# Where an extra weight row's transfers stand in the DMA queue: between the last two pieces of w2 instead of ahead of all of w2

## The chip, the cores and the metric

The kernel runs on one core of one Trainium2 chip. The metric is the device time of one execution in microseconds (us). A profile records one further execution: when each instruction ran on each engine (PE is TensorE, DVE VectorE, ACT ScalarE, POOL GpSimd, SP SyncE), when each DMA packet ran, and when each transfer's semaphore was incremented.

## The reference

One decoding step for two sequences (B = 2, one token each, model width D = 576), an attention branch and a squared-ReLU branch that read the same normalised input:

```python
x = A_x
xn = _layernorm(x, axis=-1)
return x + _A_ref(xn, k_cache, v_cache, wq, wo) + _B_ref(xn, w1, b1, w2, b2)

# _A_ref: 32 query heads on 16 key/value heads of width 128, the last W = 2048 of 8192 cached positions
p = softmax((x @ wq) k^T * Dh ** -0.5);  o = p v;  return o @ wo
# _B_ref: F = 4608
h = relu(x @ w1 + b1) ** 2;  return h @ w2 + b2
```

Everything is bfloat16. The inputs are about 54 MB, and each byte is read once: 8 tiles of k and 8 of v of 2 MB each, wq, wo and w1 of about 5 MB each, and w2 of 5 MB.

## The kernel before

**Tiles.** Loads go to tiles of 128 partitions, each partition getting one contiguous run of memory. The k and v caches come in 8 units each (`load_k(u)`, `load_v(u)`, lines 106 and 107). w2 has 4608 rows of 576. It is taken as two halves (`x=2`) of 128 partitions with 18 rows each (`FR` = 18), so that w2's row r of half x on partition p meets the transposed hidden vector `hT_sb[:, x, r, :]`:

- `w2a` is the first half, all 18 rows (line 441).
- `w2b` holds rows 0 to 8 of the second half (line 442).
- `w2c` holds rows 9 to 16 of the second half. It comes in three transfers that `W2P` lists: rows 9 to 13 (720 KB), 14 and 15 (288 KB), and 16 (144 KB) (line 444).
- `w2x_sb` holds row 17 of the second half: 128 partitions of 1152 B. This is "the extra row". It has a tile of its own that is free from the start, and it is loaded in four transfers by partitions, listed in `XS`: 85, 13, 21 and 9 of them (line 440).

**The output.** All products add up in one PSUM tile, `out_ps`, by `out_acc` (four matmuls of 144 columns each on four row groups of TensorE, line 217). The order at the end of the program on PE is fixed by program order: the last attention units, the 32 products with `wo`, the product with the extra row (line 450), the 18 products with `w2a`, then those with `w2b` and `w2c` in the order of rows. The last has `stop=True`. ACT then copies `out_ps` out (line 458) and issues the output transfer (line 459).

**The DMA queues.** Nearly all loads are issued by SP, in program order, on one queue. Each transfer is split over DMA engines, of which there are 16, and each engine works through its share of the queue in order. x, b1, b2 and the output go through ACT's queue. b1 (8 rows of 1152 B) is one transfer: `for i in range(0, 2 * NG4, 8)` runs once (line 416).

**The waits.** The tile framework hands out eight DMA semaphores in turn, over the transfers of SP and ACT together, in program order: x, k_0, b1, b2, wq, k_1, v_0, k_2, v_1, k_3 and so on. A transfer is not issued before the transfer that had its semaphore eight places earlier has landed. It also waits until the tile that it overwrites is no longer read. While SP waits for one transfer, the transfers behind it wait too. At the end of the program this gives:

- the first three pieces of the extra row wait for v_4, k_6 and v_5, the fourth for nothing new (w1)
- w2a waits for k_7, w2b for v_6, and w2c's three pieces for v_7, wo and the first piece of the extra row
- the output transfer waits for the second piece of the extra row

Of the kernel before, what the change touches and what calls it, by code (L numbers as in the profile page):

```python
# [16 lines left out]
def kernel(  # L17
# [14 lines left out]
    nc = tc.nc  # L32
    P = 128
    B, Sq, D = A_x.shape
# [26 lines left out]
    NG4 = 4  # L61
# [12 lines left out]
    FR = L1 // P  # L74
    assert HW == 32 * FR and QH * 2 == NC and NC * WC == 32
    W2P = [(0, 9), (9, 14), (14, 16), (16, 17)]
    XS = [(0, 85), (85, 98), (98, 119), (119, 128)]
    BS = 16
    MB = BS * (B - 1) + 1
    RM = 32 * (NG4 - 1) + MB  # L80
# [12 lines left out]
    def matmul(*a, **k):  # L93
        tc.keep_in_program_order(nc.tensor.matmul(*a, **k))  # L94
# [28 lines left out]
    w2x_sb = const.tile([P, D], BF16, name="w2x_sb")  # L123
# [57 lines left out]
    for t0, half, k0, n, pc in ((0, 0, 0, NK, 0), (0, 1, 0, NK, 1), (1, 0, 1, NK - 1, 1), (1, 1, 0, NK - 1, 0)):  # L181
# [11 lines left out]
                          in_=own[:].unsqueeze(2).to_broadcast([P, NC, WC]))  # L193
# [11 lines left out]
                          in_=ident[0:2 * NG4, 0:2 * NG4].rearrange("p (x g) -> p x g", g=NG4).unsqueeze(3)  # L205
                          .to_broadcast([2 * NG4, 2, NG4, B]))

    b1_sb = const.tile([2 * NG4, HW], BF16, name="b1_sb")
    w2_rows = B_w2.rearrange("(x p r) n -> x p (r n)", x=2, r=FR)
# [5 lines left out]
    def out_acc(lhsT, rhs, o, start=False, stop=False):  # L215
        for i in range(4):
            matmul(out_ps[32 * i:32 * i + MB, :], lhsT=lhsT, rhs=rhs[:, o * D + i * OQ:o * D + (i + 1) * OQ],
                   start=start, stop=stop, skip_group_check=True, tile_position=(0, 32 * i))
# [91 lines left out]
    hT_sb = const.tile([P, 2, FR, MB], BF16, name="hT_sb")  # L310
# [75 lines left out]
    def step(u):  # L386
        fin = None
        w = u - 2
        with_pv = w >= 0
        for g in range(NG):  # L390
            transposes(u, g)
            if with_pv and g == 1:
                pv(w, 0, 2)
            if with_pv and g == 2:
                pv(w, 1, 2)
                fin = pv_end(w)
            if g == TG + 1:
                scores(u, 0)
            if g == TG + 2 and fin:
                fin()  # L400
        scores(u, 1)
        softmax(u)
# [10 lines left out]
    softmax(0)  # L413
    load_v(2)
    b1_rows = B_b1.rearrange("(x n) -> x n", n=HW)
    for i in range(0, 2 * NG4, 8):
        nc.scalar.dma_start(out=b1_sb[i:i + 8, :], in_=b1_rows[i:i + 8, :])
    nc.scalar.dma_start(out=xb_sb[B:B + 1, :], in_=B_b2.rearrange("(o n) -> o n", o=1))
    step(1)
    load_k(4)  # L420
# [15 lines left out]
    r9 = W2P[0][1]  # L436
    w2b_sb = kvpool.tile([P, r9 * D], BF16, tag="kv", name="w2b")
    w2c_sb = w2pool.tile([P, (FR - 1 - r9) * D], BF16, name="w2c")
    for p0, p1 in XS:
        nc.sync.dma_start(out=w2x_sb[p0:p1, :], in_=w2_rows[1, p0:p1, (FR - 1) * D:FR * D])  # L440
    nc.sync.dma_start(out=w2a_sb[:], in_=w2_rows[0])
    nc.sync.dma_start(out=w2b_sb[:], in_=w2_rows[1, :, 0:r9 * D])
    for r0, r1 in W2P[1:]:
        nc.sync.dma_start(out=w2c_sb[:, (r0 - r9) * D:(r1 - r9) * D], in_=w2_rows[1, :, r0 * D:r1 * D])
    step(NU - 1)
    pv_all(NU - 2)
    pv_all(NU - 1)
    for r in range(WR):
        out_acc(ws[:, r, :], wo_sb, r)
    out_acc(hT_sb[:, 1, FR - 1, :], w2x_sb, 0)  # L450
    for r in range(FR):
        out_acc(hT_sb[:, 0, r, :], w2a_sb, r)
    for r in range(FR - 1):
        w, o = (w2b_sb, r) if r < r9 else (w2c_sb, r - r9)
        out_acc(hT_sb[:, 1, r, :], w, o, stop=(r == FR - 2))

# [33 lines left out]
```

## Time and profile before

| | |
|---|---|
| median of 4 runs | 134.81 us (134.71 to 135.36) |
| the profiled execution | 135.36 us |
| its span, first to last instruction | 132.9 us |
| PE busy | 86.2 us, 65% |
| DVE busy | 63.2 us, 48% |
| ACT busy | 46.8 us, 35% |
| queue q1 (SP's loads), share of 16 engines | 3618 packets, 53.61 MB, 95.1% |
| queue q8 (instructions) | 7 packets, 0.11 MB, 0.3% |
| queue q10 (ACT's transfers) | 34 packets, 0.02 MB |
| HBM read over the span | 403 GB/s |
| SP issues the extra row | 96.0 to 97.4 us |
| SP issues w2a, w2b | 97.44, 100.80 us |
| SP issues w2c's three pieces | 105.6 to 117.8 us |
| ACT starts the copy-out | 130.09 us |

The profiled execution's own time is 2.5 us longer than its span: that lies around the first and last instruction. Queue q1's share of 95.1% says that the 16 DMA engines were reading for nearly the whole span. Among the waits of SP's queue toward the end, 11.4 us are for the landing of wo and 3.0 and 4.5 us for v tiles. PE's busy time spreads over the span, and in its last part PE mostly waits for one tile of weights after another.

### The profile page before, as it was taken

Reading aid. Unit: us, or ns where it says so; the run is one execution under the profiler, and the core shown is the slowest. Engines: PE = TensorE matmul, PEld = TensorE weight load, DVE = VectorE, ACT = ScalarE, POOL = GpSimd, SP = SyncE. Lnnn points to the kernel's source line nnn. Section 1 sums busy time; section 2 is a strip of 40 time slices with the busy share of each in tenths; the row PEclk is TensorE's granted clock in tenths of the full one; section 3 lists DMA queues with packets and bytes.
Section 4 is the critical chain, followed back from the end, with each engine's and each line's share of the span. In section 5 each row is a group of like instructions: output and inputs, shape, how many; then the busy total and the mean of one; then the engine's idle time right before and its main releaser. Section 6 shows DMA issues by size and latency. Waiting matters only on the chain.

```text
span 132.9 us, 2286 instructions
## 1 busy us (share of the span) xinstructions
PE 86.2 (65%) x949; PEld 53.1 (40%) x949; DVE 63.2 (48%) x176; ACT 46.8 (35%) x67; POOL 4.9 (4%) x15
## 2 busy tenths in 40 slices
PE   0079329599688697598887697205739971659461
PEld 0069302296344353454443363003337530138350
DVE  7754400355567496547596557410165766530000
ACT  5715400339376193436174445200206632000000
POOL 5000000010000100100100100100000001000000
PEclk9999955959999999689999779855686999555955
DMA  4999899999999999999999999989999998999960
GB/s 158 394 437 522 366 404 409 459 404 439 422 439 429 439 424 419 444 414 444 414 434 431 434 431 524 442 349 414 429 434 429 435 493 377 365 406 406 414 250 1
DMA packets 3661, 53.76 MB, mean 404 GB/s; under 512 B 441, under 2 KB 708, under 8 KB 964
## 3 DMA queue, kind: packets, MB, share of 16 engines
q1 hardware_dynamic: 3618, 53.61, 95.1%
q8 instruction: 7, 0.11, 0.3%
q10 hardware_dynamic: 34, 0.02, 0.0%
q14 instruction: 2, 0.02, 0.0%
HBM read 53.62 MB, written 0.00 MB: 403 GB/s over the span
## 4 chain that ended last, share of the span: by engine, by line
DMA 72%; PE 19%; DVE 2%; ACT 2%; issue 1%; SPq 0%; POOL 0%; ACTq 0%; DVEq 0%; POOLq 0%
DMA v<-in_A_v_cache_dram 26%; DMA w2c<-in_B_w_dram 17%; DMA k<-in_A_k_cache_dram 16%; DMA wq<-in_A_wq_dram 13%; PE kT_ps L97 10%; PE sc_ps L94 3%; PE q_ps L94 3%; PE o_ps L94 1%; PE out_ps L94 1%; ACT kT L269 1%; DVE m L290 1%; DVE qrow L237 1%; DVE kT L271 1%; PE op_ps L94 1%; SPq L106 0%
## 5 line engine op out<-in xcount | busy, mean ns | idle before, releaser
L97 PE MATMUL kT_ps<-ident_f,k 128*128 128x128 f32 x256 | 42.0, 316 | 5.7 <-DMA k<-in_A_k_cache_dram 4.4
L97 PEld LDWEIGHTS kT_ps<-ident_f,k 128*128 128x128 f32 x256 | 33.4, 162 | 19.2 <-issue 10.4
L269 ACT COPY kT<-kT_ps 128x1024 bf16<-128x1024 bf16 x32 | 31.9, 1012 | 19.1 <-PE kT_ps L97 19.0
L271 DVE COPY kT<-kT_ps 128x1024 bf16<-128x1024 bf16 x32 | 21.8, 681 | 6.4 <-PE kT_ps L97 6.1
L94 PE MATMUL sc_ps<-kT,qz 128*32 128x512 bf16 x128 | 9.7, 383 | 6.6 <-DVE kT L271 4.7
L301 ACT ACTIVATE p<-sc_ps,bias 128x512 bf16<-128x512 f32 x8 | 5.5, 687 | 21.4 <-DVE gown L297 18.2
L94 PE MATMUL o_ps<-v,pT 128*32 128x512 bf16 x128 | 12.1, 462 | 0.0
L94 PEld LDWEIGHTS <-xnT 128*4 128x4 bf16 x108 | 3.5, 121 | 15.8 <-issue 14.1
L94 PE MATMUL h_ps<-w,xnT 128*4 128x288 bf16 x72 | 4.4, 438 | 7.1 <-DMA w<-in_B_w_dram 7.1
L304 DVE STREAM_TRANSPOSE pT<-p 128x512 bf16<-128x512 bf16 x8 | 5.7, 710 | 6.1 <-ACT p L301 6.1
L334 DVE SCALAR_TENSOR_TENSOR o<-o_ps,in_s,o 128x128 f32<-128x128 f32 x24 | 8.3, 344 | 0.4
L290 DVE TENSOR_REDUCE m<-sc_ps 128x1 f32<-128x512 f32 x8 | 5.5, 691 | 4.6 <-PE sc_ps L94 4.6
L94 PE MATMUL q_ps<-wq,xnT 128*4 128x512 bf16 x36 | 4.0, 627 | 4.6 <-DMA wq<-in_A_wq_dram 4.6
L374 DVE TENSOR_TENSOR hrow<-t 100x1152 bf16<-100x1152 f32 x2 | 2.6, 1356 | 8.8 <-ACT t L372 8.8
L294 POOL PARTITION_ALL_REDUCE gmax<-m x8 | 2.9, 366 | 105.1 <-DVE m L292 105.1
L458 ACT CAST fin_sb<-out_ps 113x144 bf16<-113x144 f32 x1 | 0.3, 279 | 18.4 <-PE out_ps L94 18.4
L94 PE MATMUL op_ps<-o,of_h 128*32 128x129 f32 x16 | 3.7, 316 | 4.6 <-DVE o L334 4.6
L94 PEld LDWEIGHTS <-qz 128*32 128x32 bf16 x128 | 2.1, 94 | 10.3 <-DVE kT L271 7.2
L97 PE MATMUL pro_ps<-ident,xn_sb 2*128 2x2 bf16 x5 | 0.9, 181 | 6.8 <-DVE xn_sb L172 6.5
L332 DVE TENSOR_SCALAR o<-o_ps,in_s 128x128 f32<-128x128 f32 x8 | 2.7, 343 | 5.0 <-PE o_ps L94 5.0
L94 PEld LDWEIGHTS <-hT_sb 128*17 128x17 bf16 x144 | 3.3, 106 | 4.2 <-issue 4.2
L94 PE MATMUL out_ps<-wo,ws 128*17 128x144 bf16 x128 | 4.0, 324 | 1.2 <-DVE ws L350 1.2
(72 smaller groups left out, 55.7 us busy)
## 6 DMA issues: line engine op xcount, KB each, us to landing
k<-in_A_k_cache_dram SPq DMA_DIRECT2D x8, 2048.0 KB, 21.7
v<-in_A_v_cache_dram SPq DMA_DIRECT2D x8, 2048.0 KB, 27.6
w<-in_B_w_dram SPq DMA_DIRECT2D x1, 5184.0 KB
wq<-in_A_wq_dram SPq DMA_DIRECT2D x1, 4608.0 KB, 17.7
wo<-in_A_wo_dram SPq DMA_DIRECT2D x1, 4608.0 KB, 21.8
w2a<-in_B_w_dram SPq DMA_DIRECT2D x1, 2592.0 KB
w2b<-in_B_w_dram SPq DMA_DIRECT2D x1, 1296.0 KB
w2c<-in_B_w_dram SPq DMA_DIRECT2D x1, 720.0 KB, 23.0
```

The source lines that it names most:

```text
L94: tc.keep_in_program_order(nc.tensor.matmul(*a, **k))
L97: tc.keep_in_program_order(nc.tensor.transpose(*a, **k))
L237: cp(out=qrow[:, k * QW:(k + 1) * QW].rearrange("p (i a d) -> p i a d", a=2, d=Dh), in_=q_ps[0:RB, k * QW // 2:(k + 1) * QW // 2].rearrang ...
L269: nc.scalar.copy(out=kT, in_=kT_ps[:])
L271: nc.vector.tensor_copy(out=kT, in_=kT_ps[:])
L290: nc.vector.tensor_reduce(out=m1[:], in_=sc_ps[:], axis=AX.X, op=ALU.max)
L294: nc.gpsimd.partition_all_reduce(gmax[:], m2[:], channels=P, reduce_op=ReduceOp.max)
L301: nc.scalar.activation(out=p_sb[:], in_=sc_ps[:], func=ACT.Exp, bias=bias[:, 0:1], scale=scale, accum_out=o1[:, Dh:Dh + 1])
L304: nc.vector.transpose(out=pT[:].rearrange("p j r -> p (j r)"), in_=p_sb[:])
L332: nc.vector.tensor_scalar(scalar1=in_s[:, 0:1], scalar2=None, op0=ALU.mult, **kw)
L334: nc.vector.scalar_tensor_tensor(scalar=in_s[:, k:k + 1], in1=o1[:, 0:Dh], op0=ALU.mult, op1=ALU.add, **kw)
L374: nc.vector.tensor_tensor(out=h4[:, :, k * HB:(k + 1) * HB], in0=t4, in1=t4, op=ALU.mult)
```

## The change

It does three things. The transfers of the extra row move from ahead of w2a to between the last two pieces of w2c, and are cut into 85, 25 and 18 partitions instead of 85, 13, 21 and 9. The product with the extra row moves from ahead of the 18 products with w2a to between the last two products of all. And b1 comes in two transfers of 4 rows instead of one of 8; the number of transfers over all stays what it was.

```diff
-    XS = [(0, 85), (85, 98), (98, 119), (119, 128)]
+    XS = [(0, 85), (85, 110), (110, 128)]
...
-    for i in range(0, 2 * NG4, 8):
-        nc.scalar.dma_start(out=b1_sb[i:i + 8, :], in_=b1_rows[i:i + 8, :])
+    for i in range(0, 2 * NG4, 4):
+        nc.scalar.dma_start(out=b1_sb[i:i + 4, :], in_=b1_rows[i:i + 4, :])
...
-    for p0, p1 in XS:
-        nc.sync.dma_start(out=w2x_sb[p0:p1, :], in_=w2_rows[1, p0:p1, (FR - 1) * D:FR * D])
     nc.sync.dma_start(out=w2a_sb[:], in_=w2_rows[0])
     nc.sync.dma_start(out=w2b_sb[:], in_=w2_rows[1, :, 0:r9 * D])
     for r0, r1 in W2P[1:]:
+        if r1 == FR - 1:
+            for p0, p1 in XS:
+                nc.sync.dma_start(out=w2x_sb[p0:p1, :], in_=w2_rows[1, p0:p1, (FR - 1) * D:FR * D])
         nc.sync.dma_start(out=w2c_sb[:, (r0 - r9) * D:(r1 - r9) * D], in_=w2_rows[1, :, r0 * D:r1 * D])
...
-    out_acc(hT_sb[:, 1, FR - 1, :], w2x_sb, 0)
     for r in range(FR):
         out_acc(hT_sb[:, 0, r, :], w2a_sb, r)
     for r in range(FR - 1):
+        if r == FR - 2:
+            out_acc(hT_sb[:, 1, FR - 1, :], w2x_sb, 0)
         w, o = (w2b_sb, r) if r < r9 else (w2c_sb, r - r9)
         out_acc(hT_sb[:, 1, r, :], w, o, stop=(r == FR - 2))
```

The transfers of the loop over `W2P[1:]` are rows 9 to 13, 14 and 15, and 16; `r1 == FR - 1` holds for the last, so the queue's end reads: w2a, w2b, w2c rows 9 to 13, w2c rows 14 and 15, the extra row in three, w2c row 16. By the turn of the eight semaphores, w2a now waits for v_4, w2b for k_6, w2c's first two pieces for v_5 and w1, the extra row for k_7, v_6 and v_7, the last piece for wo, and the output for w2a. From b1's second half on, each transfer is one place later in the turn: k_2 waits for x, v_1 for k_0, k_3 and v_2 for the two halves of b1, and k_4 for b2.

## The prediction

> **What bounds the kernel now.** I read the page's chain (part 4) first: DMA 72%, PE 19%, everything else 2% or less each. In the chain in order of time, the end is one transfer and what hangs on it:
>
> ```profile
> ...
> 105.63 23.04 DMA w2c<-in_B_w_dram
> 128.67 0.04 issue
> 128.72 1.35 PE out_ps L94 x26
> 130.07 0.02 issue
> 130.09 0.28 ACT fin_sb L458
> ```
>
> Columns: start, length, what. TensorE is released by a landing at 128.67, and 1.4 us later the copy-out follows. Next the timeline of PE over the end:
>
> ```profile
> ...
> 123.82 0.97 PE L94 MATMUL out_ps<-w2a,hT_sb 128*17 128x144 bf16 x49 [1.09 <-DMA w2a<-in_B_w_dram]
> 125.71 0.60 PE L94 MATMUL out_ps<-w2a,hT_sb 128*17 128x144 bf16 x23 [0.91 <-issue]
> 126.91 1.26 PE L94 MATMUL out_ps<-w2b,hT_sb 128*17 128x144 bf16 x36 [0.60 <-DMA w2b<-in_B_w_dram]
> 128.72 1.33 PE L94 MATMUL out_ps<-w2c,hT_sb 128*17 128x144 bf16 x32 [0.54 <-DMA w2c<-in_B_w_dram]
> ```
>
> Every piece of w2 is waited for. The trace's semaphore increments put the complete landings of w2c's three pieces at 128.67, 129.34 and 129.705, and the matmuls that need the third start at 129.75. So the last landing sets the end. From it to the end of the span (132.9) are 3.2 us that the change leaves alone: last product, copy-out, output transfer.
>
> Is the DMA stream full until then? Windows of the span, last column GB/s, column before it the DMA engines' busy share:
>
> ```profile
> core 0: us, PE busy (x) PEld busy (x) DVE busy (x) ACT busy (x) POOL busy (x), PEclk, DMA share, GB/s
> 106.30:110.40 4.10, 2.80 (x34) 1.26 (x32) 2.54 (x6) 1.01 (x1) 0.20 (x1) 1.00 1.00 427
> 110.40:114.50 4.10, 1.69 (x18) 0.81 (x18) 2.90 (x10) 0.78 (x2) 0.17 (x1) 0.75 0.98 423
> 114.50:117.50 3.00, 1.24 (x7) 0.18 (x2) 1.44 (x5) 0.00 (x0) 0.00 (x0) 0.50 1.01 331
> 117.50:120.60 3.10, 2.01 (x69) 2.04 (x73) 0.87 (x3) 0.00 (x0) 0.00 (x0) 0.50 1.00 428
> ...
> 126.80:129.30 2.50, 1.84 (x56) 1.62 (x56) 0.00 (x0) 0.00 (x0) 0.00 (x0) 0.50 0.65 247
> ```
>
> It is, with one dip: 331 GB/s for 3.0 us with all engines busy. That is exactly when the extra row's 128 packets of 1152 B run (first at 114.46, last at 117.0 in the packet records). A wo packet of 36864 B takes 1364 ns up to there and up to 1949 ns in the dip; a w2a packet of 20736 B takes 840 to 1133 ns in it and 771 ns from 117.5 on. The dip costs (425 - 331) / 425 x 3.0 = 0.66 us on every engine, whether it carries extra rows or not. Of these 0.66 us, the row's own 147 KB account for 0.34 us (147 KB / 431 GB/s).
>
> The last window shows the second thing to know: 247 GB/s at share 0.65, so the 16 engines don't finish together. The sixteen increments of the last piece fall at 127.9 to 128.2 (five), 128.7 to 128.8 (three), 129.2 to 129.47 (seven) and 129.705 (one). The number of increments also says how many engines a transfer used: 16 for 128 rows, but 5, 13, 7 and 9 for the pieces of 85, 13, 21 and 9 rows, each the largest divisor up to 16. The latest engine is one of the five that take 17 rows of the first piece; those five carry 17+1+3+1 = 22 of the 128 rows each. I call them row engines. The seven that follow carry at most one row, except one further row engine. The late engines without rows lost their time to instruction packets on queue q8 (16 KB each, the first at 29.6; each puts one engine 1.3 to 1.7 us behind).
>
> **The change, part by part.** The sum is made on the profiled execution: 135.36 us, span 132.9. The median of the runs shown is 134.81, 0.55 lower; I apply the difference to the median.
>
> *The move on the queue.* The engines work through their queue in order, so for each engine I can move the rows. The latest engine reads wo until 115.53 (its last packet took 1447 ns, 0.08 over normal), its 22 rows until 117.07 (1.54 us, 70 ns a row), the tiles w2a to w2c's second piece until 128.88 (11.81 us), the last 8 rows at 47 ns until 129.26; 0.445 us later comes the increment. After the change: wo until 115.45, w2 up to the second piece until 127.26, then the extra row, then 0.385 for the last piece. The new cut, by the divisors above, gives 85 = 5x17, 25 = 5x5, 18 = 9x2: 24 rows on a row engine, two more than now. The price of a row there isn't in the trace. From below, 47 ns (last piece, beside other small packets): 24 x 47 + 27 (three completion packets of 4 B, 9 ns each) = 1.155 us, so the stream ends at 128.80, 0.46 earlier. From above, 70 ns, the dip again, with the 0.08 us lost on wo and with 0.21 us lost while the early row engines run theirs (22% of the 0.95 us from 126.3 to 127.26): 115.53 + 11.81 + 0.21 + 1.71 + 0.385 = 129.64, 0.38 later. I take 50 ns, near the lower end, because the neighbours are now packets of 2304 and 1152 B, not of 20 to 36 KB, and the early engines (done by about 126.7) leave the stream: 24 x 50 + 27 = 1.23, end 128.87, 0.39 earlier.
>
> *The engines without rows.* Their last increment is at 129.465. Without the dip it is 0.66 earlier, 128.8; with all of it back, 129.47. Either way the latest row engine (128.87 + 0.445 = 129.3) is about level or later, so it sets the end.
>
> *b1 in two transfers.* Eight rows on eight engines become, by the same divisors, two on each of four engines. One more row of 47 to 70 ns on engines that probably include the latest one: 0.05 later. ScalarE issues one DMA more (0.29 like L417) after 5.19, in the shadow of the table load until 5.61; uncovered, 0.3 us would meet the 0.56 us that PE idles before k_0 lands at 8.3.
>
> *The waits on SP.* The eight DMA semaphores are used in turn, and a transfer waits for the eighth before it. b1's second half shifts this turn: v_1 now waits for k_0 (8.26 instead of 3.96), k_3 for b1's first half (about 10.6 instead of 8.27), v_2 for the second half (13.5 or so: b2, one packet further on one of b1's engines, landed at 13.48), and it is issued at 14.62 anyway. Behind them on SP stand only further loads, and wq, k_1, v_0 and k_2 keep the engines fed until 33.3. Price 0; were the queue dry, up to 4.3 us. At the end, w2a to w2c's second piece no longer wait at all (now 97.4 to 117.4), the extra row waits for k_7, v_6 and v_7 (95.9, 100.8, 105.6), and the last piece for wo as its neighbour does now (117.4), 9 us ahead of its first packet. Price 0.
>
> *The product on PE.* Four matmuls leave 122.38, where PE went on to wait 1.09 us for w2a; worth 0. In the new place they wait for the 18 rows, which land one piece (0.385 us) ahead of the last. A product takes 1.26 / 9 = 0.14 us, so it is through. Uncovered it costs 0.14. The stall of 0.91 us inside w2a (instruction packet on q8 at 123.4) moves four matmuls on; 0.60 and 0.54 us of waiting stand behind it.
>
> Sum: -0.39 + 0.05 = -0.34, so about 135.0 for the profiled execution and 134.5 for the median.
>
> A rule speaks against the change. The Trainium skill, "DMA: Bandwidth & Descriptors" (Anatomy of one DMA — SWDGE (gpsimd) path; Rules for kernel authors), gives a DMA some 2.0 us of fixed cost and calls transfers under 64 KB mostly overhead; by that, three transfers in a row before the last piece would be an estimated 6 us. The row of this trace is that w2c's second and third piece land 0.36 us apart: queued transfers overlap all but their packets, and I go by that.
>
> **Rivals.** (a) *The gain is the whole dip.* In executions without a profile the last engine may be one without rows: the profiled one is the slowest of the four, by 0.5 us. Then 0.66 us go, and a little more where rows also spare it: 134.0 to 134.15. For it: seven increments lie within 0.5 us behind the last. Against: nothing in the trace takes the two late row engines out, and they gain 0.46 at most.
> (b) *The dip moves to the end and deepens; slower.* The place is the row engines' 24 rows, now with nothing behind them but the last piece. The latest engine breaks even where (129.26 - 127.26 - 0.385 - 0.027) / 24 = 66 ns a row, and is 0.67 us late at 94 ns. For it: 70 ns was measured, in the dip. Against: the 1152 B packets of the last piece run at 47 ns on up to eight engines at once. At 70 ns with all the rest it is 135.2, at 94 ns 135.5.
> (c) *Nothing moves.* The same bytes pass, and two rows more per row engine eat the gain (60 to 66 ns a row): 134.7 to 134.9.
>
> **How the numbers follow.** 0.5% is 0.67 us here, about what a measurement of this kernel can tell from no change. Forecast 0.49 (134.25 to 134.7), (c) 0.12, (a) 0.24, (b) 0.15, of which a quarter or so stays within 0.5%. Faster by over 0.5%, under 134.15, is nearly all of (a): 0.23. Slower, over 135.48: 0.11. Same: 0.66. The range goes from (a)'s end, 134.0, to (b) at its bound with the spread of the runs, 135.3.
>
> **What would show it.** Right: no window near 331 GB/s at 114.5; the w2a product's wait ending about 0.9 us sooner (123.8 to 122.9); the extra row's product just before the last four matmuls; 1152 B packets 47 to 55 ns apart near 127 to 128.5; copy-out at about 129.75 instead of 130.09. Wrong: a window of low GB/s with full share after 126; a later copy-out with rows over 66 ns; the last landing on an engine without rows; v_2 or k_4 later than 14.6 and 33.3, or a gap in the stream before 40 us.

## The result, and the profile after

The changed kernel takes 134.59 us (median of 53 runs, 134.35 to 135.18), the kernel before 134.78 (79 runs beside them, 134.54 to 135.75). The ratio is 0.9979, with a 95% interval from 0.9971 to 0.9988. That is a gain of 0.2 us: measurable with so many runs, and well inside the 0.5% that the prediction calls "same". The forecast was 134.5.

The profiled execution after took 134.44 us with a span of 132.6 (before: 135.36 and 132.9). The chain of waits of the kernel after, in order of time, ends so (columns: start, length, what):

```profile
...
97.61 31.35 DMA w2c<-in_B_w_dram
128.96 0.04 issue
129.00 0.67 PE out_ps L94 x16
129.68 0.02 issue
129.70 0.28 ACT fin_sb L460
```

The form is the old one, a landing of w2c and a few products behind it. The copy-out starts at 129.70 instead of 130.09; the forecast was 129.75. The landing at 128.96 is that of rows 14 and 15. The last one, row 16, shows only in the semaphore increments, at 129.367 (129.705 before; forecast 129.3).

The timeline of PE over the end, of the kernel after:

```profile
118.75 4.02 PE L94 MATMUL out_ps<-wo,ws 128*17 128x144 bf16 x128 [1.16 <-DVE ws L350]
122.89 1.05 PE L94 MATMUL out_ps<-w2a,hT_sb 128*17 128x144 bf16 x54
125.37 0.48 PE L94 MATMUL out_ps<-w2a,hT_sb 128*17 128x144 bf16 x18 [1.43 <-issue]
126.00 0.74 PE L94 MATMUL out_ps<-w2b,hT_sb 128*17 128x144 bf16 x36
128.14 0.49 PE L94 MATMUL out_ps<-w2c,hT_sb 128*17 128x144 bf16 x20 [1.41 <-DMA w2c<-in_B_w_dram]
129.00 0.30 PE L94 MATMUL out_ps<-w2c,hT_sb 128*17 128x144 bf16 x8 [0.37 <-DMA w2c<-in_B_w_dram]
129.28 0.24 PE L94 MATMUL out_ps<-w2x_sb,hT_sb 128*17 128x144 bf16 x4
129.41 0.24 PE L94 MATMUL out_ps<-w2c,hT_sb 128*17 128x144 bf16 x4
```

w2a starts at 122.89 instead of 123.82. The extra row's four matmuls (second line from below) stand where the program puts them, ahead of the last four, and they add nothing: they run at 129.28, in the wait for the landing at 129.367. The stall inside w2a is still there, after 54 matmuls instead of 49, and hidden by the waits behind it.

The windows of the kernel after (last columns: granted clock, busy share of the DMA engines, GB/s):

```profile
core 0: us, PE busy (x) PEld busy (x) DVE busy (x) ACT busy (x) POOL busy (x), PEclk, DMA share, GB/s
106.30:110.40 4.10, 2.97 (x34) 1.41 (x34) 2.70 (x7) 1.01 (x1) 0.04 (x1) 1.00 1.00 427
110.40:114.50 4.10, 1.53 (x17) 0.80 (x18) 2.81 (x10) 0.78 (x2) 0.33 (x1) 0.78 0.96 416
114.50:117.50 3.00, 1.31 (x7) 0.18 (x2) 1.50 (x5) 0.00 (x0) 0.00 (x0) 0.50 0.95 407
117.50:120.60 3.10, 1.94 (x65) 1.88 (x68) 0.91 (x3) 0.00 (x0) 0.00 (x0) 0.50 1.00 431
...
126.80:129.30 2.50, 0.79 (x32) 0.50 (x32) 0.00 (x0) 0.00 (x0) 0.00 (x0) 1.00 0.49 150
```

The window with 331 GB/s has become one with 407 at a share of 0.95. A window counts a packet where it starts, and with packets of 36864 B that moves single windows by some per cent. Spread over their durations, the packet records give 431 to 433 GB/s in every half microsecond from 114.5 to 120.5. The dip in front is gone. The last window has 150 GB/s instead of 247: most engines are done earlier, and a few finish late. What these do is told by the durations of the 1152 B packets, the mean in each half microsecond of the packet records, in ns:

```
front           114.5  115.0  115.5  116.0  116.5
before             51     61     74     68     71
end             126.5  127.0  127.5  128.0  128.5
after              52     67     70     53     53
```

51 ns long (47 apart) is the undisturbed packet. So the slowed packets moved with the row, but the slow stretch became shorter: about 1.2 us (126.9 to 128.2) instead of 2 or more. The neighbours are slowed there too: the 2304 B packets of rows 14 and 15 take 122 to 124 ns in the mean between 127 and 128, and 93 ns before 126.5.

### The profile page after: what moved, and what is told of

Its sections match the earlier page's. It is cut to its first block, busy times and chain, and to the rows that moved or that the text cites. A ratio compares the mean times of both kernels' runs of the same rounds, so it can differ in the third digit from the quotient of the medians.

```text
span 132.6 us, 2285 instructions
## 1 busy us (share of the span) xinstructions
PE 83.9 (63%) x949; PEld 50.9 (38%) x949; DVE 63.3 (48%) x176; ACT 46.7 (35%) x67; POOL 4.9 (4%) x15
## 4 chain that ended last, share of the span: by engine, by line
DMA 79%; PE 13%; SPq 2%; ACT 2%; DVE 1%; issue 1%; ACTq 0%; DVEq 0%
DMA w<-in_B_w_dram 25%; DMA w2c<-in_B_w_dram 24%; DMA k<-in_A_k_cache_dram 17%; DMA wq<-in_A_wq_dram 13%; PE kT_ps L97 4%; PE h_ps L94 3%; PE q_ps L94 3%; PE sc_ps L94 1%; SPq L106 1%; PE o_ps L94 1%; ACT kT L269 1%; DVE qrow L237 1%; PE out_ps L94 1%; ACT qrow L237 0%; DVE qz L253 0%
## 5 line engine op out<-in xcount | busy, mean ns | idle before, releaser
L97 PE MATMUL kT_ps<-ident_f,k 128*128 128x128 f32 x256 | 40.7, 309 | 6.5 <-DMA k<-in_A_k_cache_dram 5.3
L97 PEld LDWEIGHTS kT_ps<-ident_f,k 128*128 128x128 f32 x256 | 32.1, 157 | 19.9 <-issue 10.4
L237 DVE CAST qrow<-q_ps 100x512 bf16<-100x512 f32 x1 | 0.7, 691 | 7.9 <-PE q_ps L94 7.9
```

Source lines behind the costliest of these rows:

```text
L97: tc.keep_in_program_order(nc.tensor.transpose(*a, **k))
L237: cp(out=qrow[:, k * QW:(k + 1) * QW].rearrange("p (i a d) -> p i a d", a=2, d=Dh), in_=q_ps[0:RB, k * QW // 2:(k + 1) * QW // 2].rearrang ...
```

## The experiments

### The row's share, and the two edits by themselves

`e1_no_row`: the kernel before without the row's transfers; the tile is set to zero, and the row's product is missing from the output.

```diff
+    nc.vector.memset(w2x_sb[:], 0.0)
...
-    for p0, p1 in XS:
-        nc.sync.dma_start(out=w2x_sb[p0:p1, :], in_=w2_rows[1, p0:p1, (FR - 1) * D:FR * D])
```

> The kernel before without the transfers of the extra row (its tile is set to zero once at the start, so this product is left out of the sum). Theory 'dip': the row's small packets slow every DMA engine between 114.5 and 117.5; without them no dip (about 425 GB/s in that window), and the seven late engines land 0.66 us sooner, so the last landing is at 128.8 instead of 129.7: 0.7 to 0.9 us faster. Rival 'only the engines that carry rows': the dip has another cause and stays, the late engines without rows still land at 129.47: 0.24 us faster.

134.35 us beside 134.82, ratio 0.9951 (0.9932 to 0.9971). The windows of this kernel:

```profile
...
114.50:117.50 3.00, 1.31 (x7) 0.18 (x2) 1.78 (x5) 0.00 (x0) 0.00 (x0) 0.50 1.01 435
...
```

No dip without the row, and the last landing at 128.633, 1.07 before that of the kernel before. On the mean engine the dip is 0.67 us (the missing GB/s of the packet records before, summed from 114.5 to 118) and the row's own bytes are 0.34, which come on top: 1.01 together. The median spans say 0.7 us (132.9 to 132.2). The time fell by 0.47 only, less than the 0.7 to 0.9 expected: the executions of this kernel lie 1.9 to 2.15 us above their spans, those of most others 1.9.

`e2_move_only`: the move of transfers and product, with the old cut (85, 13, 21, 9) and b1 in one transfer. `e3_b1_only`: b1 in two transfers, nothing else.

```diff
 e3:
-    for i in range(0, 2 * NG4, 8):
-        nc.scalar.dma_start(out=b1_sb[i:i + 8, :], in_=b1_rows[i:i + 8, :])
+    for i in range(0, 2 * NG4, 4):
+        nc.scalar.dma_start(out=b1_sb[i:i + 4, :], in_=b1_rows[i:i + 4, :])
```

> The kernel before with the transfers (old cut 85, 13, 21, 9) and the product moved, b1 in one transfer. Theory 'dip': the place is what matters, so 0.2 to 0.4 us faster, as the whole change. Rival 'cut, b1 or turn of the semaphores': no faster than before, within 0.1 us.

> The kernel before with b1 in two transfers of 4 rows, nothing else. Theory 'dip': within 0.1 us of before; v_1 issued at 8.3, k_3 at 10.7, v_2 at 14.7 and no gap in the stream. Rival 'cut, b1 or turn of the semaphores': 0.2 us faster.

The move alone: 134.63 us, ratio 0.9986 (0.9969 to 1.0003), last landing 129.504. b1 alone: 134.93 us, ratio 1.0 (0.998 to 1.002). The move has the whole effect as far as these runs can tell (its own interval still reaches just above 1), and b1's split has none that they can tell. The new cut (85, 25, 18) was not run by itself. In b1's kernel the dip is still in front:

```profile
...
114.50:117.50 3.00, 1.30 (x11) 0.23 (x3) 1.77 (x5) 0.00 (x0) 0.00 (x0) 0.50 1.00 323
...
```

Its one profile also has a second, shallower slow stretch (386 to 394 GB/s by the packet records from 120 to 122.5) that no other kernel showed; its cause stays open.

### The same bytes in one transfer

My prediction put the dip down to the row's 128 small packets. `e4_one_front` keeps the kernel before, the row's old place included, and makes the row one transfer of 128 partitions. `e5_one_tail` does the same to the changed kernel.

```diff
 e4:
-    XS = [(0, 85), (85, 98), (98, 119), (119, 128)]
+    XS = [(0, 128)]
 e5:
-    XS = [(0, 85), (85, 110), (110, 128)]
+    XS = [(0, 128)]
```

> The kernel before with the extra row in one transfer of 128 rows, in its old place ahead of w2a: 8 rows on each of the 16 engines instead of 22 on five. Tells what in the rows makes the dip. If it is rows that go to few engines (so that these write into partitions that the other engines write at the same time): no dip, every engine 0.38 us of rows, last landing near 129.2, 0.4 to 0.5 us faster. If it is any packet of 1152 B beside large ones: the dip stays, the late engines carry 8 rows more, 0.1 to 0.2 us slower.

> The changed kernel with the extra row in one transfer of 128 rows, in the new place between the last two pieces: 8 rows on each engine. Theory 'rows that go to few engines slow the others': no slow rows near the end (1152 B packets 47 ns apart throughout), the late engines land 0.38 us after where they land without any row (128.63 in the run without it), so near 129.0 to 129.25: 0.4 to 0.6 us faster than before, within 0.15 us of the same single transfer in the old place. Rival 'the place near the end is what helps': clearly faster than the single transfer in the old place, by 0.3 us or more.

In the old place: 134.38 us, ratio 0.9963 (0.9947 to 0.9979), last landing 129.248. In the new place: 134.35 us, ratio 0.9966 (0.9953 to 0.998), last landing 129.193. The windows of the first:

```profile
...
114.50:117.50 3.00, 1.31 (x11) 0.33 (x3) 2.00 (x6) 0.00 (x0) 0.00 (x0) 0.50 1.07 448
...
```

The same 128 packets of 1152 B run here in the midst of wo's and w2a's packets, and there is no dip to speak of (419 to 433 GB/s by the packet records, 0.04 us in all); every one of them takes 51 ns, in front as at the end. Once the row is one transfer, its place no longer matters as far as these runs tell, and either kernel is some 0.2 us faster than the changed one (134.59). The intervals of the ratios overlap, but all six runs of `e5_one_tail` are at or below 134.44, as only 8 of the 53 of the changed kernel are. One line of the source gives more than the whole diff.

### What of the cut does it: few engines, or foreign partitions?

One transfer differs from the old cut in two ways. All 16 engines carry 8 rows each, so none is late; and each engine writes the partitions that it writes in all other transfers of 128, if all of them are split in the same way, as I take it. Rows that go by another engine than in such a transfer I call foreign. `e9_halves_front` keeps the first and gives up the second: two transfers of 64 partitions in the old place. Each uses 16 engines (16 increments each), so every engine has 8 packets of 1152 B as in `e4_one_front`.

```diff
-    XS = [(0, 85), (85, 98), (98, 119), (119, 128)]
+    XS = [(0, 64), (64, 128)]
```

> The kernel before with the extra row in two transfers of 64 rows ahead of w2a: 4 + 4 rows on each of 16 engines, as many packets of the same size per engine as with one transfer of 128 rows, but each engine now writes partitions that belong to another engine's share of the 128-partition transfers. If the dip comes from such foreign partitions: it is back (331 GB/s or a shallower one of the same loss, 0.3 to 0.7 us), and the kernel is 0.3 to 0.7 us slower than with one transfer of 128. If it comes from the load on few engines: no dip, within 0.1 us of the single transfer.

135.03 us, ratio 1.0022 (1.0008 to 1.0036), last landing 129.979. The windows:

```profile
...
114.50:117.50 3.00, 0.86 (x3) 0.18 (x2) 2.03 (x7) 0.00 (x0) 0.00 (x0) 0.50 1.09 357
...
```

The dip is back (313 to 346 GB/s by the packet records, from 115 to 118) with the same bytes, row packets and engines: 0.65 us more than the whole transfer, and more than the kernel before. It slows the big packets of the others too, every one of them: those of wo and w2a that start between 114 and 117.6 take 1604 to 1865 and 846 to 1096 ns, where in `e4_one_front` all take 1364 and 771.

So the dip comes neither from small packets as such nor from few engines that carry them. What is left is the cut: which engine carries which row. (The second transfer as such, with its 16 more completion packets of 4 B, is an unlikely cause: at the end of `e5_one_tail` two transfers of 128 rows of 1152 B follow each other, and every packet takes 51 ns.) My reading is that it comes when engines write partitions other than their own share of a 128-partition transfer. This is argued and not shown: the records have neither the partition that a packet writes nor the address that it reads, and both change together when another engine takes a row.

The Trainium skill, "SBUF — State Buffer" (Can I just issue two DMAs to hit both halves?), says that only one transfer spanning all 128 partitions reaches all 16 ports of SBUF, and that two transfers to the halves don't make up for it. The measured 135.03 against 134.38 agrees in direction. Whether the packets contend for ports here is open: no row of these traces names a port.

`e11_halves_tail` puts the two halves in the new place.

```diff
-    XS = [(0, 85), (85, 110), (110, 128)]
+    XS = [(0, 64), (64, 128)]
```

> The changed kernel with the extra row in two transfers of 64 rows, between the last two pieces: the same balanced load as one transfer of 128 there, but foreign partitions. Ahead of w2a, two halves cost 0.65 us against one transfer (135.03 against 134.38). Theory 'foreign partitions cost less beside small packets and finished engines': 0.1 to 0.4 us slower than one transfer of 128 in this place, last landing at 129.3 to 129.6, so 134.45 to 134.75. Rival 'they cost the same anywhere': 0.65 us slower, 135.0.

134.62 us, ratio 0.9987 (0.9971 to 1.0003), last landing 129.436: 0.24 later than with one transfer in the same place, where in front it was 0.73 (129.979 against 129.248). At the end the foreign rows have small neighbours, and some engines are already done; their packets take 61 and 65 ns in the mean for one microsecond only. By the medians it is 0.27 us (134.62 against 134.35) of 0.65. This is what the move is worth: it doesn't remove the collision, it puts it where it costs a third to two fifths.

### Five engines or nine

`e7_nine_tail` cuts the changed kernel's row so that nine engines carry 14 or 15 rows each, instead of five carrying 24.

```diff
-    XS = [(0, 85), (85, 110), (110, 128)]
+    XS = [(0, 63), (63, 126), (126, 128)]
```

> The changed kernel with the row cut into 63, 63 and 2: by the divisors seen, 7 + 7 rows on nine engines instead of 24 on five. Theory 'the latest row engine sets the end': it has 9 or 10 rows less, 0.45 us at 47 ns, and is no longer last; the late engines without rows set the end between 128.8 and 129.3: 0.1 to 0.4 us faster than the changed kernel, 0.3 to 0.6 faster than before. Rival 'all 128 misdirected rows slow everyone, whoever carries them': the late engines stay where they are in the changed kernel (129.2 to 129.37), within 0.1 us of it.

134.55 us, ratio 0.9979 (0.9961 to 0.9997), last landing 129.516. Spreading the rows gained nothing that can be measured. Nine rows fewer on the heaviest engine should have brought 0.45 us at 50 ns each if its load alone set the end. Here the last landing belongs to one of the nine (129.147 for its rows of the second piece, and 0.37 us on for the last piece). Its packets can be followed back, since each starts where the one before it on its engine ends: it had its part of w2c's second piece only at 127.99, and then carried 7 and 7 rows at 47 ns. In the changed kernel the engine that ends last has that piece by 127.24. So spreading the rows also gave them to an engine that was late before.

### The product's place

`e6_product_first` has the changed kernel's transfers and the old place of the product, ahead of w2a.

```diff
+    out_acc(hT_sb[:, 1, FR - 1, :], w2x_sb, 0)
     for r in range(FR):
         out_acc(hT_sb[:, 0, r, :], w2a_sb, r)
     for r in range(FR - 1):
-        if r == FR - 2:
-            out_acc(hT_sb[:, 1, FR - 1, :], w2x_sb, 0)
```

> The changed kernel with the transfers moved, but the product with the extra row left ahead of the products with w2a. Theory 'the two moves belong together': PE stops at the product until the row lands near 129.1, and then still has 140 matmuls of w2a, w2b, w2c and the row itself, 20 to 35 ns each, and a stall for instructions of about 1 us: 3.5 to 5 us slower. Rival 'PE has time to spare at the end': the products are caught up before the last piece, under 1 us slower.

138.68 us, ratio 1.0288 (1.0267 to 1.031). The timeline of PE:

```profile
...
129.30 0.30 PE L94 MATMUL out_ps<-w2x_sb,hT_sb 128*17 128x144 bf16 x4 [6.47 <-DMA w2x_sb<-in_B_w_dram]
129.38 2.38 PE L94 MATMUL out_ps<-w2a,hT_sb 128*17 128x144 bf16 x72
131.53 1.30 PE L94 MATMUL out_ps<-w2b,hT_sb 128*17 128x144 bf16 x36
132.62 1.02 PE L94 MATMUL out_ps<-w2c,hT_sb 128*17 128x144 bf16 x32
```

PE idles 6.47 us for four matmuls, and 17 + 18 products that had stood in the waits for w2 now stand behind the last landing. The product's new place gains nothing by itself, but the transfers can't move without it.

### No tile of its own, and an accident of addresses

If the collision is the cost, the row needs no tile of its own: `e10_merged` loads rows 16 and 17 of the kernel before in one last transfer into w2c, and drops `w2x_sb`.

```diff
-    W2P = [(0, 9), (9, 14), (14, 16), (16, 17)]
+    W2P = [(0, 9), (9, 14), (14, 16), (16, 18)]
...
-    w2x_sb = const.tile([P, D], BF16, name="w2x_sb")
...
-    w2c_sb = w2pool.tile([P, (FR - 1 - r9) * D], BF16, name="w2c")
-    for p0, p1 in XS:
-        nc.sync.dma_start(out=w2x_sb[p0:p1, :], in_=w2_rows[1, p0:p1, (FR - 1) * D:FR * D])
+    w2c_sb = w2pool.tile([P, (FR - r9) * D], BF16, name="w2c")
...
-    out_acc(hT_sb[:, 1, FR - 1, :], w2x_sb, 0)
```

> The kernel before with rows 16 and 17 of w2's second half in one last transfer (128 partitions of 2304 B) and no tile of its own for row 17: no foreign partitions, one transfer and 16 completion packets fewer, the last piece twice as large (8 more matmuls wait for the last landing, 0.14 us a product). Theory: no dip, late engines end as with one transfer of 128 rows, PE's end 0.1 us later: 134.3 to 134.5, 0.3 to 0.5 us faster than before. Rival 'the extra piece costs a fixed time of its own': 0.2 us or more faster than the single transfer.

135.12 us, ratio 1.0022 (1.001 to 1.0035): slower, against every theory at hand. The time was lost long before the end. The first increment of v_7 came at 104.43 instead of 103.91, and the packet records of SP's queue give 427.2 GB/s from 40 to 104 us instead of 429.7, with the same 2.6 less from 40 to 70 as from 70 to 100. What had changed there was only where those tiles lie: without the 1152 B of `w2x_sb` all later tiles stand 1152 B lower in each partition. Two kernels tested that. `e12_merged_pad` is the merged kernel with 128 B of unused tile more, so that the shift is 1024; `e13_before_pad` is the kernel before with 384 B more, the same as 1152 less, modulo 512.

```diff
 e12, on e10:
-    const.tile([P, 112], F32, name="pad_0")
+    const.tile([P, 144], F32, name="pad_0")
 e13, on the kernel before:
-    const.tile([P, 112], F32, name="pad_0")
+    const.tile([P, 208], F32, name="pad_0")
```

> The kernel with rows 16 and 17 in one last transfer, which was slower than expected (135.12 us) because its k and v tiles loaded at 428-429 GB/s instead of 431-432. It dropped the extra row's tile, which moved every later tile down by 1152 B a partition. Here an unused tile of 128 B more is put in front, so that they move by 1024 B instead, a multiple of 512. Theory: the addresses' offset within a larger power of two is the cause: k and v are back at 431-432, v_7's first increment at 103.9-104.0 instead of 104.4, last landing 129.1-129.4, time 134.3-134.5. Rival: the addresses are not it (the turn of the semaphores or the last piece of 2304 B per partition is): stays within 0.15 of 135.1.

> The kernel before with an unused tile of 384 B a partition more in front, so that every later tile has the offset modulo 512 that the merged kernel gave it (1152 B less is 384 B more, modulo 512); transfers, order and waits are untouched. Theory that the addresses are the cause: k and v load at 428-429 GB/s, the last landing comes 0.4-0.7 us later than in the kernel before (130.1-130.4), time 135.2-135.5. Rival that they are not: within 0.15 of the kernel before.

The merged kernel went to 134.57 us, ratio 0.9983 (0.9967 to 0.9998), v_7's first increment 103.93 and 429.8 GB/s. The kernel before went to 135.76, ratio 1.0068 (1.0043 to 1.0093), v_7 at 104.48, 427.2 GB/s, a little more than expected; the dip behind it is deeper too (281 to 299 GB/s from 115.5 to 117.5, where the kernel before has 308 to 346). One window from 38 to 115 us, of the kernel before, of `e10_merged`, `e12_merged_pad` and `e13_before_pad`:

```profile
...
38.00:115.00 77.00, 54.09 (x504) 30.34 (x500) 44.57 (x110) 29.95 (x42) 2.19 (x6) 0.85 1.01 432
...
```

```profile
...
38.00:115.00 77.00, 53.73 (x508) 30.57 (x504) 44.85 (x110) 30.28 (x44) 2.19 (x6) 0.85 1.01 429
...
```

```profile
...
38.00:115.00 77.00, 53.51 (x508) 30.55 (x500) 45.12 (x111) 30.23 (x42) 2.20 (x6) 0.86 1.01 432
...
```

```profile
...
38.00:115.00 77.00, 53.10 (x503) 30.56 (x500) 44.47 (x109) 30.21 (x42) 2.20 (x6) 0.84 1.00 428
...
```

Tiles at the old offset or 1024 B from it load at 432, tiles 1152 B below it or 384 B above it at 428 to 429. That the addresses of the tiles are the cause is shown in both directions; by what step it goes isn't: the four offsets allow 256 B as well as 512, since both slow shifts are 128 B off a multiple of 256. With it set right, merging is as good as the change and no better than one transfer into a tile of its own.

## Why the prediction was right, and where not

**The dip goes: right, and its size.** 0.66 us on every engine was read off one window; the packet records give 0.67. `e4_one_front` and `e9_halves_front` differ by 0.65 us with the same row packets. That the row's own bytes are 0.34 "of these 0.66 us" was wrong, though no term of the sum used it: the GB/s of the window hold these bytes already, so they come on top. The cause I had only as "the row's packets"; it is the cut of the row, and the prediction did not see that one transfer in the old place would do more than the move.

**The price of a row: the term that was mis-sized.** I took 50 ns, "near the lower end, because the neighbours are now packets of 2304 and 1152 B". The packets of the engine that ended last (next paragraph) show its 24 rows and their three completion packets lasting until 128.56, from a start between 127.15 and 127.24: 1.32 to 1.41 us instead of 1.23, or 54 to 58 ns a row. The first 17 rows took 58 to 63 ns each, the other seven 47. So the slow price held for part of the rows, and small neighbours are slowed as well: this is the mechanism of rivals (b) and (c), and the sign "47 to 55 ns apart near 127 to 128.5" came only after 128.

**The latest row engine sets the end: right.** 129.3 was forecast and 129.367 measured. The packets of the engine that ended last can be followed back from 128.943: 8 rows and a 4 B completion packet, before them 2 rows and a completion (128.561), 5 rows and a completion (128.461), and the completion of an earlier piece at 128.22. Only a row engine carries 5 and 2 rows. Its other terms came out a little below the forecast and took up part of what the dearer rows cost: w2 up to the second piece ended between 127.15 and 127.24 instead of 127.26, the last piece took 0.38 us as forecast, and the increment came 0.42 us behind the last packet instead of 0.445. The margin was small. Two other engines ended at 128.779 and 128.758, and one of these carries no rows: I had given such engines an increment at 128.8 without the dip and at 129.47 "with all of it back", and with 0.42 to 0.51 us to the increment (129.19 to 129.29) most of it came back to them. That the row engine still came last, by 0.16 us in this one profile, was partly luck.

**b1, the waits on SP, the product: nothing, as said.** v_1, k_3 and v_2 were issued at 8.29, 10.72 and 14.66 (forecast 8.26, 10.6, 14.62), and no gap opened in the stream. b1's 0.05 us is below what `e3_b1_only` can tell. The fixed price of a DMA that the prediction weighed, and would have made 6 us, did not show: the last landings of the row's three pieces are 0.27 and 0.20 us apart.

**Rows by divisors: right.** The row's pieces of 85, 25 and 18 gave 5, 5 and 9 increments by data, the pieces of 63, 63 and 2 in `e7_nine_tail` 9, 9 and 2. The Trainium skill, "DMA: Bandwidth & Descriptors" (Why a DMA increments its semaphore by 16 and not by 1), has the rule: the largest number of engines up to 16 that divides the slowest dimension.

**Rival (a)'s argument was wrong.** I gave the whole dip 0.24 because "the profiled one is the slowest of the four, by 0.5 us", as if its last engine were later. The executions of most kernels here lie about 1.9 us above their span or about 2.4; the profiled one before was of the second kind (135.36 - 132.9). So the 0.5 us most likely lay outside the span and had nothing to do with engines.

**From the profile to the median.** The profiled span fell by 0.38 us (132.93 to 132.56), and the copy-out came 0.39 earlier; the median fell by 0.2. In the runs beside these kernels the kernel before has spans of 132.6 to 133.1 in most executions and of 133.3 to 133.6 in 21 of 94; the changed kernel has only the first kind (132.5 to 132.9). The other 73 have a median time of 134.71, still 0.12 above the changed kernel's, so a part of the gain in the median may be that the second kind is absent. What makes it is open.

## What to carry to other kernels

Load a small piece as one transfer over all 128 partitions: cut by partitions, it slowed every engine of the stream here, and the later place in the queue made up for about half of that (134.35 to 134.38 us as one transfer, 134.59 with the move, 134.78 before). Before moving a slow transfer, ask what makes it slow, and change that one thing by itself. When an edit drops or resizes a tile, compare the load rate far from the edit too, since all tiles behind it have moved.

## What the runs showed of the hardware that I had not expected

- Two transfers of 64 partitions amid large loads cost 0.65 us more than one of 128 with the same bytes and the same row packets per engine; the stream falls to between 313 and 346 GB/s from 432, and every big packet in flight is slowed.
- Moving all k and v tiles by 384 B a partition cost the kernel before 1.0 us (135.76 against 134.72; 0.6 to 1.25 by the interval of the ratio), with v_7 0.57 us later and the last landing 0.81 us later in the profiled executions (130.518 against 129.705). Moving them by 1024 B, in the merged kernel, left the rate as it was.
- The device time lies mostly either 1.9 or 2.4 us above the span, with one kernel and with another. A difference of 0.5 us between two single executions can be that alone.
